# Chunked retention ahead of two feed-forward layers: x kept on chip as two parts per layer, the running state summed in PSUM, a first group of one feature tile, and TensorE's instructions ordered from two queues

## The chip, the core and the metric

One core of one Trainium2 chip runs the whole kernel as one program. The metric is the device time of one launch in microseconds. Three timed runs of the kernel before gave 874.98, 875.25 and 876.24 us; the median is 875.25 us.

## What is computed

The reference is a retention layer (attention without softmax, with a decay per head) and two feed-forward layers, all in fp32:

```python
B, H, S, D = 4, 8, 576, 64
gamma = 1.0 - 2.0 ** (-5.0 - np.arange(H))
rel = pos[:, None] - pos[None, :]
Dmat = np.where(rel >= 0, gamma[:, None, None] ** rel, 0.0)
x = np.matmul(scale * np.matmul(q, k.transpose(0, 1, 3, 2)) * Dmat, v)     # to (B*S, H*D) = (2304, 512)
h = x @ w_in;   x = (h * sigmoid(h)) @ w_out                               # layer 1: 512 -> 2048 -> 512
h = x @ w_in2;  out = (max(h, 0) + alpha * min(h, 0)) @ w_out2             # layer 2
```

## The kernel before, in words

**Order by a planner.** Every instruction is first recorded by the class `Program` (lines 52 to 215) and not issued. `order` (line 141) then plays the recorded instructions through a table of costs per engine (`cost`, line 91; `LATENCY`, line 60) and issues them in the order in which they would start. DVE, ACT, POOL and SP take, among what is ready, the instruction with the earliest due time; PE takes its own strictly as recorded (the list `queue`, line 164). All instructions are issued at line 215, so the profile shows that line for nearly all of them, and they are told apart by their tiles. Recording is done in two parts: the first up to `close_att` (line 291), the second from there on. All engines, once the program is built, work through a fixed row of instructions, and a wait of one instruction holds up those behind it.

**Retention** works on 18 blocks of 128 tokens (two chunks of 64; nine chunks are one batch). `att_load` brings q, k (twice, in two layouts) and v of a block as two DMAs of 512 KB into one of four packs. `att_prep` multiplies v and q by decay tables (block 0 on DVE, the others on POOL); the q table is made once by `att_tables`, one DVE instruction of 2304 elements. `att_scores` makes k·q in quarters of 64x64, and `att_state` makes each chunk's k·v; both go to the PSUM tile `sd`. DVE multiplies the scores by the causal mask and adds each chunk's k·v to the running state in SBUF. `att_out` makes the output in the PSUM tile `xo`, in two units (first the part from the older state with half of the block's own part, then the other half), ACT copies each to `bufa`, and `split_block` splits it: ACT writes the high part (in type fp32r) and DVE the rest, to a ring of two pairs of x tiles.

**The layers** run over token tiles of 256, 512, 512, 512 and 512 (`TILES`) and over groups of feature tiles of 128 (`GROUPS`, line 31): layer 1 in groups of 2, 4, 4, 4, 2, layer 2 in four groups of 4. For each group and tile, `h_unit` makes one feature tile of h in one PSUM bank with 12 matmuls (4 pieces of 128 features x 3 products of high and low parts), and the nonlinearity follows on ACT and DVE. `y_unit` and `out_unit` multiply back with 3 matmuls per feature tile and add to a running sum in SBUF (`bufb`, in layer 2 `bufa`). Four banks (`bank`) go round. `split_x` splits x anew whenever a tile comes back (x tiles hold two token tiles), and every second group goes through the tiles backwards. `weight` (line 315) brings a weight tile as one DMA of 512 KB (the words lie in HBM as int64, two slots `raw`) and takes it apart into high and low part: three ACT, five DVE and one POOL instruction.

The end of the file sets the first part: blocks are recorded between the units of the first group by hand, and then `run` goes through the rest:

```python
att_next(0)
run("b", "b", "b", hs[0][0], "b", hs[0][1], "b", *ys[0], "b")
for s in range(1, len(TILES)):
    run(h[0], "b", h[1], "b")
    if s < len(TILES) - 1:
        run(y[0], "b", y[1], "b", y[2], y[3])
```

Of the kernel before, what the change touches and what calls it, by code (L numbers as in the profile page):

```python
# [18 lines left out]
P = 128  # L19
NT = B * S  # L20
# [16 lines left out]
SMALL = [C, 2 * C, C, NPAIR * C]  # L37
# [14 lines left out]
class Program:  # L52
# [4 lines left out]

    ENGINES = {"tensor": "PE", "vector": "DVE", "scalar": "ACT", "gpsimd": "POOL", "sync": "SP"}
    GRAIN = 256
    LATENCY = {"PE": 230, "DVE": 70, "ACT": 70, "POOL": 100, "SP": 1800}  # L60

# [7 lines left out]
    def __init__(self, nc):  # L69
# [7 lines left out]
        self.dma, self.was, self.started = 0.0, None, []  # L77

# [24 lines left out]
    def record(self, name, method, args, kwargs):  # L103
# [35 lines left out]
        self.ops.append((engine, name, method, args, kwargs, deps, self.cost(engine, out, reads), moved))  # L139

    def order(self):
# [21 lines left out]
        waiting = {e: set() for e in self.LATENCY}  # L163
        queue = [i for i in reversed(new) if ops[i][0] == "PE"]
# [9 lines left out]
        free, started = self.free, []  # L174
        for _ in new:
            best = None
            for e in self.LATENCY:
                if e == "PE":
                    if not queue or missing[queue[-1]]:
                        continue  # L180
                    i = queue[-1]
                else:
                    if not waiting[e]:
                        continue
                    t = max(free[e], min(ready[i] for i in waiting[e])) + 30
                    i = min((i for i in waiting[e] if ready[i] <= t), key=lambda i: (late[i], i))
                t = max(free[e], ready[i])
                if best is None or t < best[0]:
                    best = (t, e, i)
            t, e, i = best  # L190
            cost = ops[i][6]
            if e == "PE":
                queue.pop()
# [25 lines left out]
def retention_ffn_kernel(ctx: ExitStack, tc: tile.TileContext, qkv, w1, w2, alpha, small, out):  # L219
# [18 lines left out]
    bufa = big.tile([P, NC * NT], F32, name="bufa")  # L238
    bufb = big.tile([P, NC * NT], F32, name="bufb")
    oa = bufa.rearrange("p (b m) -> p b m", m=DM)  # L240
# [427 lines left out]
```

## Time and profile before

| | |
|---|---|
| median of three timed runs | 875.25 us |
| the profiled execution, its own time | 872.36 us |
| its span, from the first to the last record | 870.6 us |
| PE (TensorE matmuls) busy | 839.3 us, 96% |
| PEld (TensorE weight loads) busy | 706.3 us, 81% |
| DVE busy | 617.7 us, 71% |
| ACT busy | 429.7 us, 49% |
| POOL busy | 141.4 us, 16% |
| granted TensorE clock, mean | 0.988 |
| moved by DMA | 58.35 MB, mean 67 GB/s |

The profile is of one execution. What lies around its span is 872.36 - 870.6 = 1.8 us. "Busy" of PE is the time in which at least one matmul was under way, and matmuls overlap: the duration of one (389 ns for 128x512) is longer than the distance from one to the next, so rates are taken from the starts of neighbouring rows. A row such as `x48` merges 48 neighbouring instructions of one kind; its first number is the start of the first. Each fp32 matmul of 64x64 counts twice in the profile (the order below has it once).

### The profile page before, as it was taken

The page shows a single profiled execution, that of the slowest core. Times are in us where ns is not written, and L with a number is a line of the kernel's source. Part 1 is how long each engine was busy: PE and PEld are TensorE (multiplying, and loading weights), DVE is VectorE, ACT ScalarE, POOL GpSimd, SP SyncE. Part 2 cuts the span into 40 slices and gives each one's busy share as a digit, 9 for nine tenths or more (in the row PEclk, how much of TensorE's full clock was granted, in tenths as well). Part 3 has the DMA queues.
Part 4 walks back from the last instruction along what each step waited for, and adds up shares of the span by engine and source line. Part 5 has one row for each costly group of instructions (what it writes and reads, how often), then busy time and mean ns, then how long its engine had stood idle before and what let it go on. Part 6 is the DMA issues. An engine that isn't in the chain of part 4 may idle for free.

```text
span 870.6 us, 14570 instructions
## 1 busy us (share of the span) xinstructions
PE 839.3 (96%) x5932; PEld 706.3 (81%) x5932; DVE 617.7 (71%) x979; ACT 429.7 (49%) x819; POOL 141.4 (16%) x104
## 2 busy tenths in 40 slices
PE   4579999999999999999999999999999999999998
PEld 4467778888988888888988888888888888888887
DVE  6988569846994699646889933975449964964443
ACT  2555467524653456323654855674335753543331
POOL 4646312100220032100101100230002110200000
PEclk9789999999999999999999999999999999999999
DMA  9746513200320032100111200330002210001111
GB/s 351 257 133 203 190 50 98 73 1 25 93 78 1 25 97 78 43 1 25 49 48 49 73 1 1 97 98 1 1 0 73 73 49 1 25 0 49 49 49 72
DMA packets 17491, 58.35 MB, mean 67 GB/s; under 512 B 2064, under 2 KB 2320, under 8 KB 17424
## 3 DMA queue, kind: packets, MB, share of 16 engines
q1 hardware_dynamic: 17424, 57.43, 19.8%
q8 instruction: 46, 0.75, 0.4%
q14 instruction: 21, 0.17, 0.1%
HBM read 52.70 MB, written 4.72 MB: 66 GB/s over the span
## 4 chain that ended last, share of the span: by engine, by line
PE 94%; DVE 4%; issue 1%; ACT 0%; DMA 0%
PE bank L215 90%; PE xo L215 2%; PE sd L215 2%; DVE a L215 1%; DVE att L215 1%; DVE x L215 1%; DVE w L215 1%; DVE g L215 1%; DMA att<-in_small 0%; ACT bufa L215 0%; DVE top L215 0%; DVE bufb L215 0%; ACT low L215 0%; ACT w L215 0%; ACT g L215 0%
## 5 line engine op out<-in xcount | busy, mean ns | idle before, releaser
L215 PE MATMUL bank<-x,w 128*128 128x512 f32 (+1 forms) x1320 | 281.1, 370 | 1.7 <-ACT x L215 1.4
L215 PEld LDWEIGHTS bank<-x,w 128*128 128x128 f32 x1320 | 230.9, 189 | 44.0 <-ACT x L215 1.5
L215 POOL TENSOR_TENSOR low<-low,top 128x512 f32<-128x512 f32 x64 | 95.8, 1502 | 586.5 <-DVE top L215 551.7
L215 ACT ACTIVATE act<-bank 128x512 f32<-128x512 f32 (+1 forms) x160 | 88.4, 552 | 98.3 <-PE bank L215 95.3
L215 PE MATMUL bank<-x,w0b 128*128 128x512 f32 (+1 forms) x600 | 127.2, 368 | 0.0
L215 PEld LDWEIGHTS bank<-x,w0b 128*128 128x128 f32 x600 | 105.1, 188 | 19.1
L215 DVE SCALAR_TENSOR_TENSOR act<-down,nalpha_sb,act 128x512 f32<-128x512 f32 (+1 forms) x80 | 57.8, 722 | 68.3 <-ACT act L215 67.8
L215 ACT ACTIVATE down<-bank 128x512 f32<-128x512 f32 (+1 forms) x80 | 44.5, 556 | 107.7 <-PE bank L215 106.2
L215 PE MATMUL bank<-g,w 128*128 128x512 f32 (+1 forms) x336 | 78.8, 374 | 10.1 <-DVE w L215 6.5
L215 DVE TENSOR_TENSOR bufa<-bank,bufa 128x512 f32<-128x512 f32 (+1 forms) x55 | 37.4, 680 | 60.8 <-PE bank L215 60.8
L215 DVE TENSOR_TENSOR bufb<-bank,bufb 128x512 f32<-128x512 f32 (+1 forms) x80 | 50.5, 634 | 39.4 <-PE bank L215 39.0
L215 PEld LDWEIGHTS bank<-g,w 128*128 128x128 f32 x336 | 58.9, 197 | 21.8 <-DVE w L215 7.0
L215 DVE TENSOR_TENSOR act<-bank,act 128x512 f32<-128x512 f32 (+1 forms) x80 | 50.6, 632 | 34.2 <-ACT act L215 34.1
L215 DVE TENSOR_TENSOR g<-act,g 128x512 fp32r<-128x512 f32 (+1 forms) x84 | 60.2, 720 | 10.1 <-ACT g L215 9.7
L215 ACT CAST g<-act 128x512 fp32r<-128x512 f32 (+1 forms) x84 | 48.6, 581 | 30.0 <-DVE act L215 29.5
L215 ACT ACTIVATE top<-raw 128x512 f32<-128x512 f32 x64 | 43.0, 674 | 40.6 <-POOL low L215 40.4
L215 DVE TENSOR_TENSOR x<-bufa,x 128x512 fp32r<-128x512 f32 (+1 forms) x82 | 59.1, 744 | 4.2 <-ACT x L215 4.1
L215 PE MATMUL bank<-gb,w1b 128*128 128x512 f32 (+1 forms) x288 | 61.4, 354 | 0.0
L215 ACT ACTIVATE low<-raw 128x512 f32<-128x512 uint32 x64 | 43.0, 674 | 32.0 <-DVE w L215 14.7
L215 DVE TENSOR_TENSOR gb<-act,gb 128x512 fp32r<-128x512 f32 (+1 forms) x76 | 51.0, 673 | 9.5 <-ACT gb L215 9.0
L215 ACT CAST gb<-act 128x512 fp32r<-128x512 f32 (+1 forms) x76 | 43.9, 578 | 27.3 <-DVE act L215 27.1
L215 PE MATMUL bank<-w1b,gb 128*128 128x512 f32 (+1 forms) x252 | 55.5, 379 | 0.0
(56 smaller groups left out, 1104.3 us busy)
## 6 DMA issues: line engine op xcount, KB each, us to landing
raw<-in_w SPq DMA_DIRECT2D x64, 512.0 KB, 3.5
pack<-in_qkv SPq DMA_DIRECT2D x26, 512.0 KB, 4.8
bufb<-in_qkv SPq DMA_DIRECT2D x10, 512.0 KB, 5.3
out<-bufa SPq DMA_DIRECT2D x17, 256.0 KB, 2.0
att<-in_small SPq DMA_DIRECT2D x1, 256.0 KB, 2.8
out<-bufa SPq DMA_DIRECT2D x2, 128.0 KB, 1.7
alpha_sb<-in_alpha SPq DMA_DIRECT2D x1, 8.0 KB, 6.3
```

Of the source, the lines that this page charges most:

```text
L215: getattr(getattr(self.nc, name), method)(*args, **kwargs)
```

## The change

- `xhi` and `xlo` are two tiles that hold the high and low part of x for all tokens. ACT writes the high part straight from `xo` and DVE subtracts it from `xo`, so that `split_block`, `split_x` and the ring of x tiles fall away. In layer 1's last group `y_unit` splits its finished sum into the same two tiles. The tiles are taken in ascending order in every group.
- The running state is summed in one PSUM bank, `total`: the matmul of a chunk adds to it, and ACT copies it out per chunk. DVE's additions fall away. `bank` has 3 banks in place of 4.
- `att_half` records scores and state of half a block as one unit, quarter by quarter in turn. `att_mask` follows both halves.
- `att_prep`: v of every block on POOL, q of block 0 on DVE; the q table is made in pieces of two chunks (`att_table`). The packs are 5 (two of them in `sums`), `small` has 428 columns in place of 512.
- Layer 1's groups have 1, 3, 4, 4, 4 feature tiles.
- The planner has two queues for PE, "retention" and "layers", each a list of units; a unit, once begun, is played to its end. Among the heads of both queues it takes the one that can start first, with `SLACK` = 100 ns in favour of retention. A DVE instruction with two inputs in SBUF costs up to 1.7 times as much while POOL is busy.
- A loop records at least `LEAD` = 4 blocks ahead of the tile whose units are recorded.

```diff
-GROUPS = [(0, range(0, 2)), (0, range(2, 6)), (0, range(6, 10)), (0, range(10, 14)), (0, range(14, 16)),
-          (1, range(0, 4)), (1, range(4, 8)), (1, range(8, 12)), (1, range(12, 16))]
+SIZES = [[1, 3, 4, 4, 4], [4, 4, 4, 4]]
+LEAD = 4
-PACKS = 4
+PACKS = 5
...
+            if unit:
+                heads = [] if missing[unit[-1]] else [(max(free["PE"], ready[unit[-1]]), unit[-1], unit)]
+            else:
+                heads = []
+                for units in queues.values():
+                    if units and not any(missing[i] for i in units[-1]):
+                        t = max(ready[i] for i in units[-1])
+                        chosen = units[-1]
+                        t = max(free["PE"], t) + (self.SLACK if ops[chosen[-1]][9][0] != "retention" else 0)
+                        heads.append((t, chosen[-1], chosen))
...
+            if ops[i][8]:
+                cost += 0.7 * min(cost, max(0.0, free["POOL"] - t))
...
-    rings["bank"].grow(ps, "bank", 512, 4)
-    two = {k: ps.tile([P, 2 * 512], F32, name=k).rearrange("p (b t) -> p b t", b=2) for k in ("xo", "sd")}
+    rings["bank"].grow(ps, "bank", 512, 3)
+    total = ps.tile([P, 512], F32, name="total")
+    two = {k: ps.tile([P, 2 * 512], F32, name=k).rearrange("p (b t) -> p b t", b=2) for k in ("xo", "sc")}
...
+    def att_half(n, c):
+        nc.unit("retention")
...
+        for p in range(NPAIR):
+            for i in range(2):
+                quarter(two["sc"][rows(i), j, p * C:(p + 1) * C], k[rows(j), p, rows(i)], q[rows(j), p, rows(i)])
+                if more:
+                    quarter(total[rows(i), p * D:(p + 1) * D], k2[:, 2 * p + i], v2[:, 2 * p + i],
+                            start=g % NCH == 0 and p == 0)
+        if more:
+            states[g + 1] = rings["state"].next()
+            nc.scalar.copy(states[g + 1], total[:, 0:NPAIR * D])
...
         inside(1)
         copy(1)
-        split_block(n)
+        nc.vector.tensor_tensor(out=lo.rearrange("p (j p2) t -> p j p2 t", j=2),
+                                in0=xo.rearrange("p j (p2 t) -> p j p2 t", p2=2),
+                                in1=f32(hi).rearrange("p (j p2) t -> p j p2 t", j=2), op=ALU.subtract)
...
+        nc.vector.tensor_tensor(out=dst, in0=o, in1=dst, op=ALU.add)
+        if fs[-1] == NF - 1:
+            hi, lo = acts(xhi, at, n)[:, m], acts(xlo, at, n)[:, m]
+            nc.scalar.copy(hi, dst)
+            nc.vector.tensor_tensor(out=lo, in0=dst, in1=f32(hi), op=ALU.subtract)
...
+    att_step(-1)
+    first = [(s, u) for s in range(len(TILES)) for u in hs[s] + ys[s]]
+    at = 0
+    for i, (s, u) in enumerate(first[:-len(ys[-1])]):
+        need = sum(SPANS[s]) // P + LEAD
+        share = sum(SPANS[s][1] for s, _ in first[:i + 1]) / sum(SPANS[s][1] for s, _ in first)
+        while at < min(NBLK, max(need, LEAD + round(share * NBLK))):
+            run("b")
+            at += 1
+        u()
```

**Where instructions moved, first place: SP's loads at the start.** `att` is the table of constants, `raw` a weight tile; before, block 0 lies in `bufb`, in the change in `sums`. Before:

```order
L215 DMA att<-in_small 128x512
L215 DMA bufb<-in_qkv 128x1024 x2
L215 DMA pack_116<-in_qkv 128x1024 x2
L215 DMA pack_117<-in_qkv 128x1024
L215 DMA raw_68<-in_w 128x512
```

In the change:

```order
L249 DMA att<-in_small 128x428
L249 DMA sums<-in_qkv 128x1024
L249 DMA pack_112<-in_qkv 128x1024
L249 DMA sums<-in_qkv 128x1024
L249 DMA pack_112<-in_qkv 128x1024
L249 DMA pack_113<-in_qkv 128x1024 x2
L249 DMA sums<-in_qkv 128x1024 x2
L249 DMA pack_114<-in_qkv 128x1024 x2
L249 DMA raw_69<-in_w 128x512
L249 DMA raw_70<-in_w 128x512
```

The first half of block 1 now stands ahead of the second half of block 0, and the first two weight tiles stand behind five whole blocks.

**Second place: PE where the layers' first matmuls stand.** `x_93` and `x_94` (now `xhi`, `xlo`) are the parts of x, `w_0` and `w_1` those of the first weight. Before, in the fourth block:

```order
L215 MATMUL bank_107<-x_93,w_0_77 128x256
...
L215 MATMUL xo<-pack_118,att 64x64 x16
L215 MATMUL xo<-att,pack_118 64x64 x8
L215 MATMUL sd<-bufb 64x64 x24
L215 MATMUL xo<-att,pack_118 64x64 x8
L215 MATMUL bank_108<-x_93,w_2_79 128x256
```

In the change, in the seventh block:

```order
L249 MATMUL xo<-sums,att 64x64 x16
L249 MATMUL xo<-att,sums 64x64 x8
L249 MATMUL sc<-pack_112 64x64
L249 MATMUL total<-pack_112 64x64
...
L249 MATMUL bank_103<-xhi,w_0_77 128x256
L249 MATMUL bank_103<-xhi,w_1_78 128x256
L249 MATMUL bank_103<-xlo,w_0_77 128x256
...
L249 MATMUL xo<-att,sums 64x64 x8
...
L249 MATMUL bank_103<-xhi,w_0_77 128x256
```

Before the first dense matmul there now stand seven blocks of scores and the first unit of the sixth block's output (768 matmuls as the profile counts them); half of an h unit (6 matmuls) now stands between the two halves of an output. The last block's output stands after 24 matmuls of 256 and 72 of 512 columns.

**Third place: DVE where the second group begins.** `act` and `g` are the nonlinearity of a unit, `a`, `top`, `w0b` (in the change `w_6`, `w_7`) the steps and the parts of the third weight tile of that group. Before:

```order
L215 TENSOR_TENSOR x_94<-bufa,x_93 128x4x128 x2
L215 TENSOR_SCALAR a_75<-top_70 128x512
L215 SCALAR_TENSOR_TENSOR a_75<-top_70,a_75 128x512
...
L215 TENSOR_TENSOR act_105<-bank_107,act_105 128x512
L215 TENSOR_TENSOR a_75<-a_75,w0b_1734 128x512
L215 TENSOR_TENSOR w0b_1735<-a_75,low_74 128x512
```

In the change:

```order
L249 TENSOR_TENSOR xlo<-xo,xhi 128x4x128 x2
L249 TENSOR_TENSOR act_101<-bank_105,act_101 128x512
L249 TENSOR_TENSOR g_94<-act_101,g_93 128x512
L249 TENSOR_SCALAR a_75<-top_71 128x512
L249 SCALAR_TENSOR_TENSOR a_75<-top_71,a_75 128x512
...
L249 TENSOR_TENSOR a_75<-a_75,w_6_83 128x512
L249 TENSOR_TENSOR w_7_84<-a_75,low_73 128x512
```

The third weight of the second group was taken apart right behind the last split of x, and now stands behind the nonlinearity of the first group's last h unit (`act_101`, `g_94`). On PE, between that h unit and the first matmul of this weight, stand 24 matmuls of 256 and 12 of 512 columns.

## Rows read from the trace of the kernel before

**Rows 1.** The page: the span, PE's line, and PE's clock in 40 slices.
```profile
span 870.6 us, 14570 instructions
...
PE 839.3 (96%) x5932; PEld 706.3 (81%) x5932; DVE 617.7 (71%) x979; ACT 429.7 (49%) x819; POOL 141.4 (16%) x104
...
PEclk9789999999999999999999999999999999999999
```

**Rows 2.** Four stretches: length, each engine's busy time and instructions, clock, DMA.
```profile
core 0: us, PE busy (x) PEld busy (x) DVE busy (x) ACT busy (x) POOL busy (x), PEclk, DMA share, GB/s
0.00:28.00 28.00, 15.27 (x496) 14.23 (x496) 18.07 (x26) 9.14 (x18) 15.01 (x16) 0.88 0.88 326
28.00:49.70 21.70, 11.27 (x216) 9.79 (x210) 20.48 (x28) 9.82 (x21) 13.79 (x11) 0.70 0.57 200
49.70:115.20 65.50, 60.51 (x1653) 48.46 (x1652) 49.35 (x74) 34.86 (x69) 27.74 (x23) 0.99 0.53 172
115.20:867.40 752.20, 752.20 (x3584) 633.83 (x3576) 529.39 (x851) 375.92 (x711) 84.91 (x56) 1.00 0.14 44
```

**Rows 3.** PE in order of time: start, duration, engine, line, tiles, count.
```profile
101.14 0.69 PE L215 MATMUL xo<-pack,att 64*64 64x64 f32 x32
...
103.17 3.02 PE L215 MATMUL bank<-x,w 128*128 128x512 f32 x12
...
218.90 3.04 PE L215 MATMUL bank<-x,w0b 128*128 128x256 f32 x24
221.78 3.04 PE L215 MATMUL bank<-x,w 128*128 128x256 f32 x24
...
266.30 11.04 PE L215 MATMUL bank<-x,w 128*128 128x512 f32 x48
277.18 1.52 PE L215 MATMUL bank<-gb,w1b 128*128 128x512 f32 x6
```

**Rows 4.** The same view where PE stood longest; idle time and releaser in brackets.
```profile
45.15 4.64 PE L215 MATMUL bank<-g,w 128*128 128x256 f32 x20 [4.32 <-DVE w L215]
```

**Rows 5.** The stretch ahead of the first fall of the clock, and the three lower ones, as rows 2.
```profile
13.00:16.40 3.40, 1.30 (x59) 1.03 (x54) 3.30 (x7) 2.03 (x4) 1.29 (x2) 1.00 1.03 416
16.40:19.80 3.40, 2.94 (x99) 2.75 (x102) 2.50 (x5) 1.75 (x4) 3.40 (x3) 0.50 1.03 420
...
23.20:26.60 3.40, 3.40 (x69) 3.28 (x61) 2.92 (x5) 2.09 (x5) 2.32 (x3) 0.50 0.67 192
...
36.90:50.50 13.60, 6.07 (x51) 5.42 (x53) 12.67 (x16) 3.75 (x8) 7.83 (x6) 0.50 0.32 111
```

**Rows 6.** All engines in order of time, at the start.
```profile
3.58 2.56 DVE L215 TENSOR_TENSOR att<-att 128x2304 f32<-128x2304 f32 x1 [2.70 <-DMA att<-in_small]
...
6.92 1.99 PE L215 MATMUL sd<-bufb 64*64 64x64 f32 x64 [6.92 <-DVE bufb L215]
```

**Rows 7.** The first two stretches of 5 us, as in rows 2.
```profile
0.00:5.00 5.00, 0.00 (x0) 0.00 (x0) 1.50 (x2) 1.50 (x2) 0.20 (x4) 1.00 0.64 181
5.00:10.00 5.00, 1.99 (x64) 1.80 (x64) 3.52 (x5) 0.00 (x0) 1.38 (x2) 1.00 1.00 376
```

**Rows 8.** All engines in order of time, around one copy out of `xo`.
```profile
101.66 0.41 PE L215 MATMUL xo<-att,pack 64*64 64x64 f32 x16
...
102.14 0.37 ACT L215 COPY bufa<-xo 128x256 f32<-128x256 f32 x1 [0.29 <-PE xo L215]
```

**Rows 9.** Groups of instructions, 0 to 116 us: count, busy us, mean ns, idle.
```profile
L215 POOL TENSOR_TENSOR pack<-pack,att 128x512 f32<-128x512 f32 x25 | 32.8, 1319 | 30.8 <-DMA pack<-in_qkv 25.8 <-PE sd L215 2.8 <-PE xo L215 1.2
...
L215 DVE TENSOR_TENSOR att<-sd,att 128x512 f32<-128x512 f32 x18 | 12.4, 687 | 9.6 <-PE sd L215 9.5
...
L215 ACT CAST w<-a 128x512 fp32r<-128x512 f32 x8 | 5.0, 621 | 4.4 <-DVE a L215 4.4
```

**Rows 10.** DVE in order of time, one weight's first and last step.
```profile
119.46 0.43 DVE L215 TENSOR_SCALAR a<-top 128x512 int32<-128x512 int32 x1 [2.34 <-ACT top L215]
...
124.41 0.69 DVE L215 TENSOR_TENSOR w0b<-a,low 128x512 fp32r<-128x512 f32 x1
```

More of the change, by code (lines that the diff above doesn't have):

```diff
@@ L138, in record @@
         moved = int(np.prod([c for _, c in out.ap])) * np.dtype(mybir.dt.np(out.dtype)).itemsize if engine == "SP" else 0
-        self.ops.append((engine, name, method, args, kwargs, deps, self.cost(engine, out, reads), moved))
+        shared = engine == "DVE" and len(reads) > 1 and all(r.space != bass.MemoryType.PSUM for r in reads)
+        self.ops.append((engine, name, method, args, kwargs, deps, self.cost(engine, out, reads), moved,
+                         shared, (self.queue, self.units)))
     def order(self):
@@ L162, in order @@
         users, missing, ready = {i: [] for i in new}, {}, {}
-        waiting = {e: set() for e in self.LATENCY}
-        queue = [i for i in reversed(new) if ops[i][0] == "PE"]
+        waiting = {e: set() for e in self.LATENCY if e != "PE"}
+        queues = {}
+        for i in reversed(new):
+            if ops[i][0] == "PE":
+                queue, unit = ops[i][9]
+                units = queues.setdefault(queue, [])
+                if not units or ops[units[-1][-1]][9][1] != unit:
+                    units.append([])
+                units[-1].append(i)
         for i in new:
@@ L173, in order @@
                 waiting[e].add(i)
-        free, started = self.free, []
+        free, started, unit = self.free, [], None
         for _ in new:
             best = None
[L177 to L186, printed above, removed]
+            for e in waiting:
+                if not waiting[e]:
+                    continue
+                t = max(free[e], min(ready[i] for i in waiting[e])) + 30
+                i = min((i for i in waiting[e] if ready[i] <= t), key=lambda i: (late[i], i))
                 t = max(free[e], ready[i])
@@ L189, in order @@
                     best = (t, e, i)
+            if unit:
[8 more added lines that the diff above has]
+                        heads.append((t, chosen[-1], chosen))
+            if heads:
+                t, i, chosen = min(heads, key=lambda h: h[:2])
+                t = max(free["PE"], ready[i])
+                if best is None or t < best[0]:
+                    best = (t, "PE", i)
+                    if not unit:
+                        unit = chosen
+                        next(units for units in queues.values() if units and units[-1] is chosen).pop()
+                    unit.pop()
             t, e, i = best
@@ L371, in att_state @@
[L371 to L380 removed]
+        v = heads(n, 3)
@@ L407, in mm @@
             half = p % 2
-            nc.tensor.matmul(xo[rows(half), j, c ^ j, p // 2], lhsT, rhs,
-                             start=(j, half) not in begun, stop=True, skip_group_check=True)
+            quarter(xo[rows(half), j, p // 2 * P + c * C:p // 2 * P + (c + 1) * C], lhsT, rhs,
+                    start=(j, half) not in begun)
             begun.add((j, half))
+        nc.unit("retention")
         for c in range(2):
@@ L508, in y_unit @@
             weight(layer, 1, f)
+        nc.unit("layers")
         o = psum()[:, 0:n]
```

194 lines of the change are left out of this document (80 added, 114 removed).

## The prediction, made before the changed kernel was run

> **What bounds the kernel now.** I read the page first. The span is 870.6 us and PE is busy in 96% of it; its clock is below full only at the start [rows 1]. So I cut the span into stretches [rows 2]: from 115.2 to 867.4 us PE is busy in 752.20 of 752.20 us. No wait can be taken out there, only matmuls, and the change keeps all of them. Up to 115.2 us PE is busy for 15.27 + 11.27 + 60.51 = 87 us, partly at a lower clock. The opening is where time can be won.
>
> How much, comes from the distance between starts [rows 3]. 48 matmuls of 512 columns take 277.18 - 266.30 = 10.88 us, 226.7 ns each; 24 of 256 take 221.78 - 218.90 = 2.88 us, 120 ns each. One block of retention (128 matmuls) takes 103.17 - 101.14 = 2.03 us. By the loops there are 3156 matmuls of 512 columns and 600 of at most 256; of the 5932 on PE [rows 1] that leaves 2176 for retention, 17 full blocks (chunks without an older state have fewer). The work is 3156 x 0.2267 + 600 x 0.120 + 17 x 2.03 = 715.4 + 72.0 + 34.5 = 821.9 us. PE ends at about 867.4 us [rows 2], so 45.5 us are lost: by the order of the instructions 656 matmuls of retention (10.4 us) and 48 of 256 columns (5.8 us) are done at 49.7 us, so 33.5 us go there; another 11.5 go between 49.7 and 115.2 us, where 11.9 blocks and 132 matmuls of 512 columns (54.0 us) take 65.5; the remaining 0.5 come later.
>
> The 33.5 us have three visible parts: PE starts at 6.92 us [rows 6]; the first y units wait for weights that DVE takes apart (the longest wait is 4.32 us, and PE is busy for only 11.27 of 21.70 us around it [rows 2, 4]); and three stretches, 20.4 us in all, run at half clock with PE busy for 2.94 + 3.40 + 6.07 = 12.4 us in them, of which half, 6.2 us, is lost [rows 5].
>
> **The change part by part.** *Dense matmuls, y additions and the end of the program* stay, so 821.9 us of work and the 3.2 us behind PE's last matmul stay. The splits of x that fall away were hidden under a full PE after 115.2 us: worth nothing there.
>
> *Start.* Block 0's second half is now SP's fourth transfer, behind 0.22 + 3 x 0.52 = 1.79 MB with itself. 0.9 MB are moved by 5 us and 376 GB/s follow [rows 7]: it lands at 5 + 0.88 / 0.376 = 7.4 us. POOL multiplies v after that, 1.3 us [rows 9], and the first unit needs it: PE starts at about 8.7 us, 1.8 later than now [rows 6]. The smaller table on DVE (512 elements for 2304, some 1.9 of the 2.56 us [rows 6]) doesn't help, since the transfer is later.
>
> *Retention alone, up to the first dense matmul.* The cycle from block to block is a chain: the first output unit, 101.66 + 0.41 - 101.14 = 0.93 us to its end; 0.07 to ACT; a copy of 0.37 [rows 3, 8]; then the second unit, 0.41 with 0.07 ahead of it; again 0.07 and 0.37; then DVE's subtraction, 0.69 as the like instruction that reads PSUM and SBUF [rows 9], with 0.07 on both sides. That makes 3.1 us. Beside it run the scores and the state of the next block, the mask (0.69 on DVE) and two copies of the state on ACT (0.37 each); they fit into the gaps. Loads and POOL are faster than the chain: 1.05 MB per block at 376 GB/s and up are 2.8 us or less [rows 7], 2 x 1.32 us on POOL are 2.6 [rows 9]. The bounds are 2.6 us (loads and POOL alone set it) and 4.2 us (the chain's matmuls at half clock, and DVE late by half an instruction each time); I take 3.1, since the weights, which hold DVE up, are two here and not four. The first output starts 3.1 us after PE: half a block of scores and state, a quarter of 2.03 us and 0.15 more to its end; the state's copy, 0.51 with both hand-overs; the other half, 0.65; the mask, 0.83; the next block's first half, 0.51. That is 11.8 us, the sixth output starts at 11.8 + 5 x 3.1 = 27.3, and the first dense matmul 80 matmuls (1.2 us) later, at 28.5 us. Done by then are 768 matmuls of retention, six blocks, 12.2 us. Lost: 16.3 us.
>
> *Retention and first group together.* Left are 11 blocks (22.3 us) and, up to the last block's output, 24 matmuls of 256 and 72 of 512 columns (19.2 us), 41.5 us. The same mixture lost 11.5 on 54.0 us before, 21% [rows 2]. DVE has less to do per block (the two additions of the state and the dearer split go), but there is less dense work in the gaps; I keep 21%, so 8.7 us. Bounds: 10%, 4.2 us (half, as DVE is freed), and 40%, 16.6 us (the first 49.7 us lost two thirds, so a stretch near that mixture may lose this much). The waits of 4.32 us for the weights of the first y units go, since the first group needs two weights, not four, and its y units stand later; late next is the subtraction out of `xo`, which is in the chain.
>
> *Second group.* Its third weight now stands on DVE behind the last h unit of the first group. From the end of that unit: sigmoid, product, cast and the weight's first ACT step, four of 0.62 to 0.69 us [rows 9] with 0.07 each, 2.9 us; then the weight's DVE steps, 125.10 - 119.46 = 5.6 us with other work between them [rows 10]. PE has 24 x 0.120 + 12 x 0.2267 = 5.6 us of cover. The wait is between nothing (half of the 5.6 us is other work that isn't there) and 2.9 us; I take 1.8, nearer the row than nothing.
>
> *Three banks.* A unit now waits for the evacuation of the unit three before it, not four. At 512 columns and three or more features that leaves two units, at least 2 x 9 x 0.2267 = 4.1 us; the evacuation itself takes some 0.7. Only the tile of 256 is tight (2 x 9 x 0.120 = 2.2 us). I cost it at nothing; the cover is gone if DVE lags by more than that (third rival).
>
> *Sum.* Lost: 16.3 + 8.7 + 1.8 + 0.5 = 27.3 us against 45.5, so 18.2 less. The profiled execution, 872.4 us, would become 854.2. The timed runs lie 2.9 us above it (875.25 us in the median), so the predicted time is **857 us**.
>
> **A rule that speaks against it.** The rows show the clock at 0.50, the 1.2 GHz level, in three stretches; in the 3.40 us ahead of the first, PE was busy for 1.30 us [rows 5]. In the change PE does retention alone for 20 us. The Trainium skill, "TensorE: Matmul & The Clock Gate", section "HAM oscillation — how this bites in real kernels", says that idle gaps between bursts of matmuls put the clock back to the lower level, so that each burst starts slow. By that rule this opening would run at half clock; no run here has that opening yet. It is the first rival.
>
> **The rivals.** *The clock falls.* If retention alone runs at 1.2 GHz, the matmuls of the chain add 0.93 + 0.41 us at most, cut to about 1.1 where the waits absorb some, so 4.2 us a block: 5 x 1.1 + 1.5 for the first block is 7 us, and some 2 us on the next stretch as retention is further behind: 866 us. For it: the lower clock at 16.4 and 23.2 us in the same part of the program [rows 5]. Against it: there loads were waited for, while here the chain keeps PE at 2.03 of 3.1 us, with gaps of under 1 us. A new wait for a weight of up to 4.32 us [rows 4] would lead to the same time.
>
> *The opening follows the loads.* With 2.6 us a block (2.5 us less), PE's start as before (1.8 less), half the loss in the mixture (4.4 less) and no wait in the second group (1.8 less): 847 us. For it: five packs let loads run further ahead, and ACT takes the state's copies off DVE.
>
> *Slower, by the banks.* Place: the 256-column tile at the start of groups 2 to 9, eight visits, where the next group's weights crowd DVE too. PE waits there for DVE's lag less 2.2 us. Before, with four banks and four features, PE never waited up to a lag of 3 x 12 x 0.120 = 4.3 us [rows 2, 3]. A lag of 4.3 us at every visit costs 8 x 2.1 = 17 us and eats the gain; above 4.7 us it is slower: at 5.0, 8 x 2.8 = 22 us and 879 us. For it: DVE is busy for 529 of 752 us [rows 2] and its fixed row can't give way. Against it: that a lag so long never showed, and DVE loses the repeated splits.
>
> **How the numbers follow.** Forecast 0.60 (857, 850 to 864), clock or a new wait 0.17 (866), loads 0.14 (847), banks 0.09 (879, from 874 on). The range 847 to 869 takes the forecast, half of the loads' case and three quarters of the clock's; 0.20 is left out. A measurement here can tell 0.2%, 1.75 us: faster is under 873.5, slower over 877.0. The other three cases lie under 873.5 but for 0.03 of the clock's; the banks' case gives 0.03 to "same" and 0.06 to "slower". Faster 0.88, same 0.06, slower 0.06.
>
> **What would show it.** In the profile after: PE's first matmul near 8.7 us; first dense matmul near 28.5 us; output units of blocks 1 to 5 some 3.1 us apart, waiting for DVE's subtraction; the last retention matmul near 79 us; full clock throughout the opening; from there PE busy without a gap but for one of 1 to 3 us in the second group. Wrong: a clock of 0.50 between 10 and 28 us, PE waiting for a weight in the first group, or waits of `bank` for DVE or ACT in the tile of 256.

## The result, and the profile after

The changed kernel takes **879.52 us** (median of 7 runs, 877.88 to 881.09) against 875.25 of the kernel before (7 runs, 872.85 to 876.24): ratio 1.0054, 95% interval 1.0039 to 1.0068. It is slower by half a per cent. Predicted were 857 us, with 0.06 for slower.

The page of the changed kernel, with the line of q8, a DMA queue that fetches instructions:

```profile
span 879.3 us, 14312 instructions
...
PE 849.7 (97%) x5932; PEld 713.6 (81%) x5932; DVE 543.4 (62%) x838; ACT 384.0 (44%) x721; POOL 137.2 (16%) x105
...
PEclk9799999999999999999999999999999999999999
...
q8 instruction: 46, 0.75, 0.3%
```

The profiled execution took 881.09 us, 1.6 above its median, and that of before 872.36, 2.9 below its own: of the 8.7 us between the two traces, 4.5 are the choice of executions.

The stretches of [rows 2] in the changed kernel, the third cut at 80 us (length, busy time and instructions of each engine, clock, DMA share, GB/s):

```profile
0.00:28.00 28.00, 14.07 (x432) 12.86 (x432) 9.70 (x14) 7.23 (x17) 13.89 (x17) 1.00 0.86 311
28.00:49.70 21.70, 16.61 (x489) 14.85 (x492) 15.52 (x22) 10.61 (x26) 13.56 (x12) 0.69 0.76 264
49.70:80.00 30.30, 29.46 (x816) 22.94 (x807) 24.50 (x35) 19.68 (x48) 22.79 (x18) 1.00 0.72 249
80.00:115.20 35.20, 28.55 (x614) 22.54 (x605) 12.91 (x21) 15.62 (x36) 3.61 (x3) 0.90 0.18 62
115.20:867.40 752.20, 752.19 (x3564) 632.80 (x3563) 477.81 (x744) 330.87 (x598) 83.35 (x57) 1.00 0.13 44
```

And the kernel before over the two middle ones:

```profile
49.70:80.00 30.30, 26.89 (x681) 20.94 (x684) 28.56 (x40) 16.62 (x34) 16.46 (x14) 0.99 0.61 194
80.00:115.20 35.20, 33.62 (x984) 27.52 (x977) 20.79 (x35) 18.23 (x36) 11.28 (x10) 1.00 0.47 153
```

From 115.2 us on PE is as full as before; DVE is busy there for 478 us in place of 529 and ACT for 331 in place of 376, which is worth nothing under a full PE, as predicted. The loss is in the opening again. I count it as the prediction did: time less the matmuls started by then, at 226.7 ns, 120 ns and 2.03 us a block. Up to 80 us both kernels lose the same, 40.1 us after and 40.4 before. From 80 to 115.2 us the change loses 13.1 and the kernel before 4.6. That is the net loss. And the 18 us that were to be won before 80 us aren't there.

The start (all engines in order of time; idle time and releaser in brackets):

```profile
7.31 0.69 DVE L249 TENSOR_TENSOR sums<-sums,att 128x512 f32<-128x512 f32 x1 [3.19 <-DMA sums<-in_qkv]
8.04 0.69 DVE L249 TENSOR_TENSOR att<-att 128x512 f32<-128x512 f32 x1
8.05 0.47 PE L249 MATMUL sc<-sums 64*64 64x64 f32 x2 [8.05 <-DVE sums L249]
8.81 1.26 POOL L249 TENSOR_TENSOR pack<-pack,att 128x512 f32<-128x512 f32 x1 [8.37 <-DVE att L249]
10.03 1.04 POOL L249 TENSOR_TENSOR sums<-sums,att 128x512 f32<-128x512 f32 x1
11.13 0.37 PE L249 MATMUL total<-sums 64*64 64x64 f32 x1 [2.60 <-POOL sums L249]
```

PE begins at 8.05 us and stops after two matmuls: it waits for v of block 0, which POOL multiplies from 10.03 us on. Two things end just ahead of that. On POOL, q of block 1 is done at 10.07 (it waited for a table piece that DVE makes at 8.04). And v's half of block 0 lands only at 9.9 us; this is its transfer, issued at 2.1 us, with the time from issue to landing:

```profile
L249 SPq DMA_DIRECT2D sums<-in_qkv x1: 432/432/432, 2.1 to 2.1; - x1
...
DMA to landing us min/median/max: 7.8/7.8/7.8
```

PE goes on at 11.13 us. Its three longest gaps from there to 112 us, and a shorter one of the same kind:

```profile
21.41 0.39 PE L249 MATMUL xo<-pack,att 64*64 64x64 f32 x5 [1.32 <-issue]
...
30.85 0.38 PE L249 MATMUL xo<-sums,att 64*64 64x64 f32 x3 [0.68 <-issue]
...
41.70 0.38 PE L249 MATMUL xo<-att,sums 64*64 64x64 f32 x5 [2.06 <-issue]
...
87.01 0.39 PE L249 MATMUL xo<-pack,att 64*64 64x64 f32 x5 [3.22 <-issue]
```

None of these four waits for an engine (the longest gap that does is 0.79 us, at 14.65). "Issue" is time in which PE waited for nothing that the profile shows; all such gaps up to 116 us add up to 8.9 us, against 4.5 before. Here are stretches of constant clock around them:

```profile
30.60:37.30 6.70, 5.83 (x178) 5.40 (x181) 4.95 (x7) 2.28 (x6) 3.50 (x3) 0.50 0.95 353
...
40.80:47.50 6.70, 5.80 (x96) 5.11 (x99) 2.98 (x5) 2.90 (x7) 5.04 (x4) 0.50 0.41 127
47.70:85.10 37.40, 34.24 (x1051) 27.17 (x1044) 27.39 (x41) 23.83 (x58) 25.35 (x20) 1.00 0.75 263
85.20:91.90 6.70, 4.89 (x75) 3.73 (x78) 0.69 (x1) 0.75 (x2) 0.00 (x0) 0.50 0.02 4
```

The gap of 2.06 us ends at 41.70 and the clock is at 0.50, the 1.2 GHz level, from 40.8 to 47.5; the gap of 3.22 us ends at 87.01 and it is at 0.50 from 85.2 to 91.9. Of the 13.1 us from 80 to 115.2, gaps of over 0.3 us make 6.6, the lower clock 2.4 (half of 4.89 busy), and six changes from 64x64 matmuls to dense ones and back, at some 0.22 us beyond the matmuls' own distance, 1.3. Some 2.8 are not accounted for.

### The profile page after: what moved, and what is told of

The parts are those of the page before. It is cut to its first block, busy times and chain, and to the rows that moved or that the text cites. A ratio compares the mean times of both kernels' runs of the same rounds, so it can differ in the third digit from the quotient of the medians.

```text
span 879.3 us, 14312 instructions
## 1 busy us (share of the span) xinstructions
PE 849.7 (97%) x5932; PEld 713.6 (81%) x5932; DVE 543.4 (62%) x838; ACT 384.0 (44%) x721; POOL 137.2 (16%) x105
## 4 chain that ended last, share of the span: by engine, by line
PE 94%; DMA 2%; DVE 1%; issue 1%; POOL 1%; ACT 1%; SPq 0%; POOLq 0%; DVEq 0%
PE bank L249 90%; PE xo L249 2%; DMA sums<-in_qkv 1%; PE sc L249 1%; PE total L249 1%; POOL sums L249 1%; DVE att L249 0%; POOL pack L249 0%; DMA pack<-in_qkv 0%; DVE a L249 0%; DVE act L249 0%; POOL low L249 0%; DVE xlo L249 0%; ACT act L249 0%; DVE sums L249 0%
## 5 line engine op out<-in xcount | busy, mean ns | idle before, releaser
L249 PE MATMUL bank<-xhi,w 128*128 128x512 f32 (+1 forms) x880 | 252.3, 372 | 0.5 <-ACT xhi L249 0.5
L249 PEld LDWEIGHTS bank<-xhi,w 128*128 128x128 f32 x880 | 160.6, 190 | 28.9 <-ACT xhi L249 0.6
L249 PE MATMUL bank<-xlo,w 128*128 128x512 f32 (+1 forms) x440 | 163.0, 370 | 0.0
L249 DVE TENSOR_TENSOR sums<-bank,sums 128x512 f32<-128x512 f32 (+1 forms) x135 | 88.2, 653 | 93.0 <-PE bank L249 91.4
L249 PE MATMUL bank<-xhi,w0b 128*128 128x512 f32 (+1 forms) x400 | 113.2, 368 | 0.0
L249 PEld LDWEIGHTS bank<-xlo,w 128*128 128x128 f32 x440 | 83.7, 190 | 14.4 <-DVE xlo L249 0.4
L249 PEld LDWEIGHTS bank<-xhi,w0b 128*128 128x128 f32 x400 | 72.6, 189 | 12.6
L249 PE MATMUL bank<-xlo,w0b 128*128 128x512 f32 (+1 forms) x200 | 73.6, 368 | 0.0
L249 PE MATMUL bank<-g,w 128*128 128x512 f32 (+1 forms) x300 | 67.2, 373 | 1.1 <-DVE act L249 1.1
L249 PEld LDWEIGHTS bank<-g,w 128*128 128x128 f32 x300 | 51.5, 189 | 10.8 <-DVE act L249 1.5
```

What stands on the lines that cost most here:

```text
L249: getattr(getattr(self.nc, name), method)(*args, **kwargs)
```

## The experiments

Times are medians beside the kernel before on the same chip (873.5 to 875.0 us), so ratios are what to compare; the change itself has 1.0054. Differences between two runs are given in us by their ratios (0.0010 is 0.87 us). A diff is against the changed kernel.

**Group size, queues, clock, loads.**

```diff
-SIZES = [[1, 3, 4, 4, 4], [4, 4, 4, 4]]
+SIZES = [[2, 4, 4, 4, 2], [4, 4, 4, 4]]
```

> The changed kernel with layer 1's groups as before (2, 4, 4, 4, 2), all else kept. Filler theory (one feature tile leaves retention too little dense work from 80 us on, where 13.1 of the 54 us are lost): those 13.1 us fall to about 5, and the time to about 872 us. Clock theory (retention alone runs at 1.2 GHz until 27 us, at 5.0 us a block): nothing changes before the first dense matmul, the loss up to 50 us stays at 34 us, and the time stays within 878 to 881. Supply theory (loads, POOL and PE's instruction fetch set the pace): as the clock theory, or slower by up to 4 us as four weights are taken apart early.

Measured: 886.49 us, 1.0138 (1.0111 to 1.0166), slower than the change. That is slower than any of the three theories allowed. More dense work beside retention doesn't help, for PE waits 6.4 us in one place, for a weight (`w`) and for products of the nonlinearity (`g`) that stand among the steps of the four weights. PE's waits from 45 to 56 us:

```profile
PE bank L249 <- DVE g L249: 2.4, 2, 2.3
PE bank L249 <- DVE w L249: 2.2, 1, 2.2
PE bank L249 <- ACT g L249: 1.8, 1, 1.8
```

```diff
-        self.queue = queue
+        self.queue = "layers"
```

> The changed kernel with TensorE's units played from one queue, in the order in which they were recorded. If the order from two queues is what costs (dense units come too late or too scattered): the loss up to 115 us falls from 53 us to near 45, and the time to 872. Clock and supply theories: the retention blocks come at the same pace of 5.0 us until the first dense unit, and the time is 877 to 883, as recorded dense units stand in larger pieces and hold retention up.

Measured: 898.2 us, 1.0256 (1.0217 to 1.0294). That is above both expectations: the two queues are worth 18 us and are not what costs.

```diff
+    cold = rings["g"].tiles[7]
+    nc.vector.memset(f32(cold), 0.0)
+    for _ in range(18):
+        nc.tensor.matmul(rings["bank"].tiles[2], cold[:, 0:P], cold, start=True, stop=True)
     att_step(-1)
```

> The changed kernel with 18 extra matmuls of 128x512 on a zeroed tile at the start of TensorE's row, where it has nothing else to do until 8 to 11 us; their result is never read. Clock theory: scores and state run at 14.6 to 16 ns per matmul in place of 27 from the first block on, blocks come 3.1 to 3.8 us apart in place of 5.0, the first dense matmul at 33 to 36 us in place of 43, and the time falls by 6 to 9 us to 870 to 873. Supply theory: the matmuls are faster but wait longer, blocks stay at 4.5 to 5 us, the time falls by 0 to 2 us.

Measured: 880.06 us, 1.0065 (1.0041 to 1.0090), as the change. The clock is up from 5.9 us and falls again:

```profile
5.90:12.60 6.70, 3.00 (x43) 2.13 (x41) 2.07 (x3) 0.14 (x1) 3.60 (x3) 1.00 1.01 372
12.80:19.40 6.60, 5.33 (x168) 4.98 (x169) 2.94 (x5) 1.89 (x6) 4.47 (x4) 0.50 1.03 419
19.60:29.60 10.00, 5.82 (x257) 4.91 (x254) 4.64 (x8) 5.56 (x13) 7.35 (x7) 1.00 0.83 294
```

From 19.6 to 29.6 us, now at the upper level, 257 matmuls of retention are done, two blocks in 10 us; the change did as many from 20 to 30. PE's gaps put down to issue add up to 12.0 us here, in place of 8.9: it is faster and waits longer. So the lower clock at the start alone is not what sets the pace.

```diff
     def att_load(n):
+        if n >= PACKS:
+            return
```

> The changed kernel without the loads of q, k and v from the sixth block on: the packs keep the first five blocks' data, so the output is not the reference's. Supply theory: with 13.6 MB less to move the blocks from the sixth on come at 3.1 us or faster, PE's waits without a visible releaser (7.5 us, five times) go, and the time falls by 8 us or more, to 871 or less. Clock theory: the first five blocks and their clock stay, only the waits without a releaser and the lower clock behind them go, 3 to 5 us, to 874 to 876.

Measured: 874.88 us, 1.0003 (0.9986 to 1.0020), 4.5 us less than the change. The issue gaps fall from 8.9 to 2.2 us. But the planner, which no longer sees these loads, also chose another order.

**The row held fixed.** From here on some runs leave instructions out when they are issued, while the planner still counts them. So every engine keeps the row that it has in the change.

```diff
         for i in self.order():
+            if i in self.left:
+                continue
```

The first leaves out the DVE and POOL steps of the first seven weights, the second POOL's products, the third both and the loads of blocks 5 to 17. The first and the third also clear tiles on DVE up to 6.3 us; its first product isn't held up by that (6.91 us there, 7.31 in the change).

> Leaves out the five DVE steps and the POOL step of the seven weights that are taken apart in the first part of the program (their low parts stay at zero, their high parts are not made from the loaded words); everything else stays in the row it has in the changed kernel, since the planner still counts the steps. Theory A (DVE's fixed row sets the pace: the mask and the subtraction out of xo stand behind weight steps of 0.9 to 1.8 us): the blocks before 26 us, where no weight step stands yet, keep their pace of 5.0 us, those behind it fall to 3.3 to 3.8 us, and the time is 868 to 872 us. Theory B (loads, POOL's products and late instruction fetches set the pace, DVE only fills its waits with weight steps): the pace stays at 4.5 to 5 us and the time at 876 to 880.

> Leaves out POOL's products of q and v with the decay tables for blocks 1 to 17; the row of every engine is otherwise that of the changed kernel. Theory A (DVE's row): DVE's weight steps fall from 0.9 to 1.8 us to their length without POOL beside them (0.42 to 0.69), so the pace behind 26 us falls to 3.5 to 4 us, and the blocks before 26 us, which waited for POOL's products, gain too: first dense matmul near 36 us, time 866 to 871. Theory B (loads and instruction fetches set the pace): the early blocks gain POOL's 2 us once, the pace stays at 4.5 us or more, time 875 to 878.

> Leaves out three things at once: the DVE and POOL steps of the first seven weights, POOL's products for blocks 1 to 17, and the loads of blocks 5 to 17 (old data are used). What is left of retention is PE, ACT's copies, the mask and the subtraction, in the changed kernel's own row. If the chain I counted is right (3.1 us a block), the first dense matmul comes at 29 to 31 us and the time is 853 to 859 us. If the pace stays at 4 us or more, the chain itself, as the two queues lay it out, is longer than counted, and the time is over 866.

Measured: 879.65 us, 1.0057 (1.0036 to 1.0078); 878.40, 1.0048 (1.0031 to 1.0065); 867.61, 0.9921 (0.9899 to 0.9943). Theory A falls: without DVE's steps, or without POOL's products, nothing is won, though DVE is busy for 3.46 us in place of 11.43 from 28 to 43 us in the first. Issue gaps are 11.5 and 8.4 us there, and 2.1 with the loads gone. The bare chain isn't 3.1 us either: the first six output units of the third run start 3.88 us apart. One of its cycles at the upper clock, all engines:

```profile
30.57 0.38 ACT L254 CAST xhi<-xo 128x256 fp32r<-128x256 f32 x1
30.98 0.69 DVE L254 TENSOR_TENSOR xlo<-xo,xhi 128x512 fp32r<-128x512 f32 x1 [0.60 <-ACT xhi L254]
...
31.72 0.46 PE L254 MATMUL xo<-pack,att 64*64 64x64 f32 x16 [0.60 <-DVE xlo L254]
...
32.98 0.28 PE L254 MATMUL xo<-att,pack 64*64 64x64 f32 x3 [0.58 <-issue]
```

Output units start at 24.84, 28.18, 31.72 and 35.47 us, 3.34, 3.54 and 3.75 apart; the two distances ahead of them are 3.64 and 5.13, the latter with a gap of 1.17 put down to issue. Behind the first unit stands half a block of scores and state, 0.68 us, where I had counted only the copy (0.44), and even without loads the gap put down to issue is there.

**The start alone:** block 0 as one transfer, its v on DVE.

```diff
+        if n == 0:
+            nc.sync.dma_start(out=pack(n), in_=qkv[n])
+            return
...
-        nc.gpsimd.tensor_tensor(out=v, in0=v, in1=vtab[:, n % PERIOD].unsqueeze(2).to_broadcast([P, H, D]), op=ALU.mult)
+        engine.tensor_tensor(out=v, in0=v, in1=vtab[:, n % PERIOD].unsqueeze(2).to_broadcast([P, H, D]), op=ALU.mult)
```

> Keeps the whole computation. Block 0 is loaded by one transfer, ahead of block 1, and its v is multiplied on DVE and not on POOL, as in the kernel before. PE's first unit should start without its wait of 2.6 us for POOL, at 8.5 to 9 us in place of 11.1. Theory A and B alike give 877 to 878 us if the blocks behind keep their distance; if the loads set when the later blocks can go, the first dense matmul stays at 43 us and the time at 879.

Measured: 876.51 us, 1.0026 (1.0008 to 1.0043), some 2.5 us of the loss back. PE goes on at 8.64 us, 2.5 earlier. The run changes the transfer and the engine at once, so it doesn't tell how much is due to which:

```profile
8.64 0.37 PE L249 MATMUL total<-sums 64*64 64x64 f32 x1 [0.86 <-DVE sums L249]
```

**The order of the halves.**

```diff
             att_half(m, 0)
-        next(out)
-        if m < NBLK:
+            att_state(m, 0)
             att_half(m, 1)
             att_mask(m)
+        next(out)
+        if m < NBLK:
+            att_state(m, 1)
```

> Keeps the whole computation. Both halves of the next block's scores and state are recorded ahead of a block's two output units (the second state copy behind the first of them), so no half stands between the output units any more. Theory C (the cycle of a bare block is 4.2 us, as seen with everything else left out: subtraction, first output unit, half a block of scores and state, second output unit, copy, subtraction): the cycle loses the half's 0.68 us less the 0.44 us of the copy that it covered, and the mask no longer stands ahead of the subtraction; with loads and products beside it the pace goes from 5.0 to about 4.4 us, the first dense matmul comes near 39 us, time 874 to 877. If late instruction fetches and the clock set the pace, whatever the order: 878 to 880.

> The edit before together with the start of an earlier run (block 0 as one transfer, its v on DVE), which alone gave 876.5. Theory C: the two add up, 871 to 874 us. Rival: they win the same time, since what is won at the start is waited for again at the loads: 876.

> The same order of units with the three things left out (steps of the first seven weights, POOL's products and the loads of blocks 5 to 17), which in the changed kernel's order gave 867.6 us. Theory C: the bare pace falls from 4.2 to 3.1 to 3.6 us a block, first dense matmul at 31 to 34 us, time 859 to 863. If the time stays at 866 to 868, the half between the output units was not in the cycle.

Measured: 884.85 us, 1.0121 (1.0094 to 1.0149); 878.90, 1.0053 (1.0036 to 1.0070); 870.61, 0.9953 (0.9932 to 0.9973). As a way to a faster kernel the theory falls: all three times lie above what either side expected, and each is slower than its counterpart in the change's order. Of the chain it is right in part: in the bare run, once the clock is on record, two units start 3.14 and 3.33 us apart (27.20, 30.34, 33.67), the first by the 3.1 us of the prediction's chain, in its steps; but over the first six units the mean is 3.86 us, as in the change's order (3.88).

```profile
28.66 0.46 PE L254 MATMUL xo<-att,pack 64*64 64x64 f32 x16 [0.49 <-ACT xhi L254]
...
29.59 0.69 DVE L254 TENSOR_TENSOR xlo<-xo,xhi 128x512 fp32r<-128x512 f32 x1 [1.39 <-ACT xhi L254]
...
30.34 0.69 PE L254 MATMUL xo<-sums,att 64*64 64x64 f32 x32
```

With loads beside it a gap ends that. In the whole computation PE stood for 2.61 us ahead of 35.83, and the clock was at 0.50 behind it:

```profile
26.70:36.80 10.10, 5.47 (x255) 4.67 (x247) 6.70 (x11) 4.64 (x12) 7.10 (x6) 1.00 0.93 331
36.90:43.60 6.70, 6.10 (x120) 5.49 (x123) 5.06 (x6) 4.08 (x9) 4.11 (x3) 0.50 0.81 256
```

**What the gaps are.** I counted PE's matmuls ahead of each gap put down to issue (but for those of 0.3 to 0.6 us at the first matmul of a half, where another unit begins):

| kernel | matmuls ahead of the gap (length, us) |
|---|---|
| before | 221 (1.60), 348 (2.10), 1872 (0.77) |
| change | 220 (1.32), 475 (0.68), 601 (0.21), 728 (2.06), 1871 (3.22) |
| 18 matmuls more at the start, counted with them | 220 (1.54), 347 (0.70), 475 (0.46), 728 (2.51), 982 (0.48), 1490 (0.98), 1871 (2.09) |
| loads of blocks 5 to 17 left out, row held | 220 (1.22), 728 (0.16), 1872 (0.25) |

They stand at the same count of matmuls, whatever the work there, the kernel or the time (18 more at the start don't move the count), and 126 to 127 matmuls apart or a multiple (1871 - 728 = 9 x 127). Queue q8 moves 46 packets and 0.75 MB in all, 16 KB each [the page above]; PE's 5932 matmuls and 5932 weight loads make 258 instructions to a packet, about 64 bytes each. So a packet would hold some 127 matmuls with their weight loads, one block of retention; that q8 carries PE's instructions is inferred from this. In dense work the same packet lasts 127 x 0.2267 = 29 us. The Trainium skill, "Runtime: NRT & Kernel Launch", section "Instruction fetch mechanics", says that an engine's instructions come in blocks of 16 KiB, 256 instructions, by a DMA queue of its own, and that crossing a boundary is mostly hidden. The spacing agrees; hidden it is not here, with up to 3.22 us. In the trace of the change a packet of q8 starts ahead of each of the five gaps, at 19.09, 28.57, 33.52, 39.32 and 84.61 us, takes 0.92 to 0.96, and PE goes on 1.36 to 1.45 us behind its end each time (21.41, 30.85, 35.92, 41.70, 87.01). Each of the five started 2.97 to 4.26 us after PE had passed the place 127 matmuls ahead of its gap.

**Fewer packs.**

```diff
-PACKS = 5
+PACKS = 3
```

> Keeps the whole computation. Three packs in place of five, so that at most three blocks' loads run ahead. If the gaps that the profile puts down to issue (8.9 us up to 115 us in the changed kernel, always at the same places of PE's row, one block's instructions apart) are instruction fetches held up behind queued loads, they shrink to under 5 us in all and the time is 874 to 877, unless a block now waits for its load. If the blocks do wait for loads, PE waits for POOL's product at each block and the time is 880 to 885.

Measured: 883.23 us, 1.0102 (1.0072 to 1.0132). The issue gaps are 7.7 us, hardly less. The time lies where waits for loads were expected: from 10 to 116 us POOL waits 32.8 us for loads in place of 13.5, and PE 7.5 us for POOL in place of 5.0. The planner also chose another order (first dense matmul at 27.51 us), so this run doesn't test the packs alone. Once PE waits for the subtraction, which stands behind a weight step on DVE, and the lower clock comes after it again:

```profile
54.65 0.46 PE L249 MATMUL xo<-pack,att 64*64 64x64 f32 x16 [1.97 <-DVE xlo L249]
```

```profile
55.90:62.60 6.70, 5.67 (x133) 4.46 (x132) 4.04 (x7) 2.43 (x6) 3.42 (x4) 0.50 0.51 159
```

**Only the loads.** The row is held; left out are the loads of blocks 5 to 17, then those of blocks 14 to 17 alone.

```diff
+        nc.leave = n >= PACKS
         nc.sync.dma_start(out=pack(n)[:, 0:2], in_=qkv[n, :, 0:2])
         nc.sync.dma_start(out=pack(n)[:, 2:4], in_=qkv[n, :, 2:4])
+        nc.leave = False
```

> Leaves out only the loads of blocks 5 to 17 (old data are used); every engine keeps the row of the changed kernel otherwise. Theory D (loads in flight hold up PE's instruction fetches, and each gap of over 1.3 us puts the clock to its lower level behind it): the gaps put down to issue fall from 8.9 us to under 3, the clock stays at its upper level from about 25 us on, and the time is 868 to 871 us, nearly that of the run with all three things left out (867.6). If the gain needs DVE's and POOL's steps gone as well: 874 to 877.

> The same, for the loads of blocks 14 to 17 alone, which in the changed kernel are issued from 67 to 79 us. Theory D: the opening up to 65 us stays as it is, the gap of 3.2 us at 84 us shrinks to under 1.2 us and the lower clock from 85 to 92 us goes: 3.2 - 1.0 + 2.5 = 4.7 us, time 874 to 876. If that gap is none of a fetch held up by loads, it stays and the time is 878 to 880.

Measured: 872.19 us, 0.9976 (0.9964 to 0.9989), and 876.90, 1.0036 (1.0019 to 1.0054). The first is 6.8 us below the change, a little less than expected, and faster than the kernel before. All issue gaps of PE up to 116 us are 2.0 us there, 6.9 less than in the change; the three at output units:

```profile
21.22 0.39 PE L254 MATMUL xo<-pack,att 64*64 64x64 f32 x11 [1.22 <-issue]
...
36.91 0.29 PE L254 MATMUL xo<-att,sums 64*64 64x64 f32 x5 [0.16 <-issue]
...
80.46 0.34 PE L254 MATMUL xo<-pack,att 64*64 64x64 f32 x8 [0.25 <-issue]
```

The fetches start earlier, too: of the twelve packets of q8 from the third on, the latest starts 1.92 us after PE passed the place one packet ahead; of the same twelve in the change, five start 2.97 to 4.26 us after. The packets themselves take 0.9 to 1.4 us without these loads, 0.9 to 1.7 with them. So what the loads change is the start of a fetch.

The run without the late loads keeps the opening's gaps, and only the last one shrinks, from 3.22 us to 0.22; behind it the clock stays up:

```profile
87.16 0.35 PE L254 MATMUL xo<-pack,att 64*64 64x64 f32 x9 [0.22 <-issue]
```

```profile
75.70:115.20 39.50, 35.37 (x810) 27.84 (x805) 19.50 (x32) 22.10 (x50) 6.49 (x6) 1.00 0.05 16
```

It wins 1.6 us, not the 4.7 expected, and the two intervals overlap: the trace shows that the gap and the lower clock behind it are gone, the time doesn't show what that is worth. The length of such a gap differs from run to run, and the profiled execution of the change is its slowest.

**On the whole computation:** the start with LEAD = 2, with four packs, and with a block's load in four transfers of 256 KB (four packs, five packs).

```diff
-        nc.sync.dma_start(out=pack(n)[:, 0:2], in_=qkv[n, :, 0:2])
-        nc.sync.dma_start(out=pack(n)[:, 2:4], in_=qkv[n, :, 2:4])
+        for i in range(4):
+            nc.sync.dma_start(out=pack(n)[:, i], in_=qkv[n, :, i])
```

> Keeps the whole computation. The start of the earlier run (876.5 us by itself) and LEAD of 2 in place of 4: the first two weights are loaded ahead of the fourth block, and the first dense matmul stands behind four blocks and not seven. Theory D: with dense work between the units a block's worth of instructions lasts longer, so fewer fetches come late; first dense matmul near 29 us, time 871 to 875. If the layers' work then catches up with the blocks and waits for them or for weights, the gain is given back: 876 to 880.

> Keeps the whole computation. The same start with four packs in place of five. Fewer loads run ahead, the first two weights come one block earlier. Theory D: 873 to 876 if the gaps shrink with the queue of loads; 877 to 880 if blocks wait for loads, as with three packs (883.2).

> Keeps the whole computation: the start and the four packs of the run before (875.6 us), and a block's load as four transfers of 256 KB, one per part (2 KB to a partition), in place of two of 512 KB. If a fetch waits behind the packet that each DMA engine has under way, shorter packets shorten the gaps put down to issue, above all the one of 2.65 us at 33 us with the lower clock behind it: 870 to 873 us, faster than the kernel before. If a fetch waits behind all that is queued, the gaps stay as they are: 875 to 877.

> The same with five packs, to be set against the run with the start alone (876.5 us). Shorter packets help: 871 to 874; all that is queued counts: 876 to 878.

Measured: 880.53 us, 1.0075 (1.0056 to 1.0094); 875.56, 1.0027 (1.0013 to 1.0041); 876.19, 1.0020 (1.0005 to 1.0035); 877.31, 1.0037 (1.0021 to 1.0053). Dense work at 30 us and not 40 doesn't help; the gaps stay (9.4 us with the start alone, 10.5 with LEAD = 2, 12.0 with four packs), though the time with four packs lies where shrinking gaps were expected. Shorter packets don't shorten them (12.0 to 11.8 with four packs, 9.4 to 12.9 with five). No run on the whole computation beats the kernel before. Why a fetch starts late when loads are queued isn't settled: neither shorter packets nor one or two packs fewer took the gaps away, and these runs changed the planner's order too.

## Why the prediction was wrong

| loss, us | predicted | measured |
|---|---|---|
| up to the first dense matmul | 16.3 (at 28.5) | 30.8 (at 42.98) |
| from there to the last block's output | 8.7 | 20.4 |
| behind it | 2.3 | 2.9 |
| sum | 27.3 | 54.1 |

- **Start, 8.7 us: mis-sized, 11.13.** Two terms of it were wrong. The half with v landed at 9.9 us and not at 7.4: what lands at 7.2, and starts DVE's product at 7.31, is the half with q. By 9.9 us 247 GB/s x 9.9 us, 2.4 MB, had been moved; the 1.79 MB counted up to that half were not moved first and alone. And I left out POOL's queue, where q of block 1 ends at 10.07. Either of the two would have held v up until 10 us. With v on DVE again and block 0 as one transfer PE goes on at 8.64 us, and the kernel is some 2.5 us faster.
- **Retention alone, 3.1 us a block: this step failed.** The first dense matmul came 14.5 us later than predicted: 3.8 up to the first output unit (15.55 for 11.8, the late start in it), 7.8 in the five distances behind it, and 2.9 in the 80 matmuls after that (4.15 us for 1.2, with the gap of 2.06 in them). The first six output units start 4.66 us apart (15.55 to 38.83; 4.67 in the run without the late loads), beyond the upper bound of 4.2. What the bounds left out is PE's own supply: a block of 64x64 matmuls uses up one fetch of instructions, and with loads queued, that fetch comes late. That is shown by leaving out the loads alone: 4.01 us a block (15.89 to 35.94), gaps of 2.0 us for 8.9, and 6.8 us less in all. That takes away 0.65 of the 1.56 us that a block was over the prediction. DVE's steps and POOL's products left out as well take 0.13 more. The last 0.78 (3.88 for 3.1) stay without all three, and what makes them up is only shown in part: the fetch gap of 1.17 us in one of the five distances, half a block of scores and state between the two output units (0.68 for the 0.44 counted), and the lower clock from 21.7 to 25.1 us in that run. PE's gaps of 4.5 us at the same matmuls are in the trace of before, too; the prediction has no term for them.
- **The mixture, 21%: mis-sized.** It lost 20.4 us on 41.5, beyond my upper bound of 16.6. The end of it is the net loss: the late fetch at 84 us, 3.22, and the lower clock behind it, 2.4; 2.8 us there are not accounted for.
- **Full clock in the opening: wrong, as the first rival had it**, 20.5 us at the lower level behind the first record at 27.1 us. But the rival's cause, bursts that start slow, is not shown to be the bound: in the run with 18 matmuls more, retention from 19.6 to 29.6 us went no faster at the upper level, and the time was the same. That run raised the clock only up to 12.6 us, so what an opening at the upper level throughout would take isn't shown. Two of the three lower stretches stand at the gaps of 2.06 and 3.22 us.
- **Loads faster than the chain, 2.8 us a block: true as a supply, and the error all the same.** Loads were costed for the data that they bring and not for the fetches that come late beside them.
- **Three banks at nothing: right.** PE is busy for 752.19 of 752.20 us behind 115.2. The rival that ended on the slower side fell; the kernel got slower by another way.
- **The second group's wait, 1.8 us:** PE's one longer wait there is 1.08 us, for a nonlinearity and not for the third weight.

That DVE's work on weights, POOL's products and the loads together cost 11.6 us (867.61), but the first two nothing as long as the loads are there, is measured; that they would bound the next version is only argued.

## What to carry to other kernels

Count the instructions of a stretch of small matmuls as a load of their own: here 16 KB of them held 2 us of 64x64 matmuls, and PE waited up to 3.2 us for a fetch that came late beside the loads of data. Gaps put down to "issue" that return after the same number of matmuls show it, and a run with the loads left out and the row held tells what they cost. Look up for each transfer when it landed, and which half of a block it brought. Don't take a chain's length as the pace unless the row that the planner lays out has nothing else between its links.

## What was not expected of the hardware

- PE's gaps at multiples of 126 to 127 matmuls with their weight loads, 0.2 to 3.2 us; all gaps put down to issue add up to 8.9 us with loads queued and to 2.0 without those of blocks 5 to 17.
- Four gaps of 2 to 3 us in a busy stretch were each followed by 6.7 us at the 1.2 GHz level (40.8 to 47.5 and 85.2 to 91.9; 36.9 to 43.6 and 55.9 to 62.6 in two other runs). The one at 84 us so costs 3.22 + 2.4 us. But the length of a gap alone doesn't tell: behind one of 2.02 us in the run with the halves and the start the clock stayed at 1.00, and behind one of 1.04 us at 82.96 in the run with the start alone it was at 0.50 from 84.3 to 87.5. So the 1.3 us of theory D are not borne out.

```profile
86.45 0.21 PE L249 MATMUL sc<-sums 64*64 64x64 f32 x1 [2.02 <-issue]
```

```profile
86.50:100.00 13.50, 12.63 (x344) 9.63 (x347) 5.25 (x8) 6.93 (x16) 0.00 (x0) 1.00 0.02 4
```

- Ahead of the first record of the clock, at 27.1 us of the change, the profile shows 1.00. That can't be relied on: 31 matmuls there take 1.10 us, and 32 of the same kind take 0.69 elsewhere [rows 3].

```profile
25.34 1.10 PE L249 MATMUL xo<-pack,att 64*64 64x64 f32 x31
```
